# The y^T products of a unit joined to the next unit's first level, a planner that counts changes of product kind, and weight loads that wait on a semaphore

## The chip, the cores and the metric

One core of a Trainium2 chip. The metric is the device time of one launch in microseconds (us); the kernel before has a median of 994.12 us over 3 runs (993.74, 994.12 and 997.86).

## The reference

A recurrent attention over 768 time steps for 4 x 8 heads of width 48, then two feed-forward layers on its 3072 x 384 output, all in float32:

```python
for t in range(S):
    cur = einsum('bhd,bhe->bhde', u[None] * kt, vt)
    y[:, :, t] = einsum('bhd,bhde->bhe', rt, state + cur)
    state = wt[:, :, :, None] * state + einsum('bhd,bhe->bhde', kt, vt)
x = y as (3072, 384)
x = (x @ w_a) * (x @ w_b) @ w_out            # 384 -> 1536 -> 384
h = x @ w_in                                 # 384 -> 2048
out = (max(h, 0) + alpha * min(h, 0)) @ w2_out
```

The weights arrive as 64-bit floats and are made into float32 pairs on the chip.

## The kernel before

**Attention.** The recurrence is cut into 12 units (6 stretches of 128 time steps, two halves of the batch each). In a unit, VectorE builds the products inside blocks of 4, 8 or 16 time steps (`natural`, L577), which go through a small DRAM buffer into the diagonal blocks of a matrix M (`diag`, L642). The blocks beyond the diagonal come level by level: `tree` multiplies decays into the tile Tp on VectorE, and `level` (L682) makes the block products on TensorE into `psl`, which ScalarE copies into M. The first level is h = 4, 8 or 16; from unit 4 on it is 16, with 128 small products, followed by level 32 with 64. Then come `ktrans` (8 transposes into `psk`), `dstate` (64 products into `psd`), the state update, and `yout` (L840): twice 64 products of M and Z into `psx`, the transposed output y^T, one for each half b. ScalarE and VectorE turn each `psx` into the two-part operand X of the first feed-forward layer.

**Feed-forward.** Two units make a block of 512 columns. `mlp1` runs, for each block, 12 steps of nine products into `pa`, nine into `pb` and nine into `acc`, each a 128x128 weight against 512 columns in the reduced float32 format (fp32r). ScalarE copies `pa` out, VectorE multiplies, both split the result. `mlp2` does likewise with the tiles `hp`, `hb` and `acd`. So TensorE does two kinds of product: the attention's small ones in float32, and the feed-forward's large ones in fp32r. In the profile all large ones have line L919.

**Weights.** `load_w` (L412) loads a weight on the Pool queue (`raw`, L432); ScalarE and VectorE make it into `w` (L437 sign, L449 exponent, L443 low part, L452 join, L458 first half, L399 rest). At most 6 loads may be ahead of the making: before a load, GpSimd copies one element of the weight made 6 places earlier into `tick` (L431), and the load stands behind this copy on the Pool queue.

**Order.** Nothing in the code is in its final order. Each piece of work is added to a list with its engine, an estimated duration, a priority, what it reads and writes, and a buffer. `Tasks.run` (L336) simulates the list forwards, takes due times from a backward pass, repeats this 8 times, keeps the order with the earliest simulated end, and issues the pieces in that order; on the chip each engine then works through its own pieces strictly in that order. The accumulators `psk`, `psd`, `psx` and `psl` share a pool of three PSUM banks. Until the first `pa`, idle TensorE time is filled with products of no use (`warm`).

Of the kernel before, what the change touches and what calls it, by code (L numbers as in the profile page):

```python
# [7 lines left out]
F32 = mybir.dt.float32  # L8
# [66 lines left out]
class Tasks:  # L75
# [26 lines left out]
    def add(self, eng, dur, prio, fn, r=(), w=(), alloc=None, nbytes=0, work=0, packet=3072, kind="", late=0.0):  # L102
# [32 lines left out]
            self.late[i] = late  # L135
        return i

    def forward(self, prio):
        import heapq

# [25 lines left out]
        runs = []  # L166
        done = [0.0] * n
        taken = {}

        for i in range(n):  # L170
            if not need[i]:
# [32 lines left out]
        while left:  # L204
            progress = True
            while progress:
                progress = False
                for eng, q in ready.items():
                    if busy.get(eng, 0.0) > now + 1e-9 or not q:
                        continue  # L210
                    q.sort()
                    for k, (p, i) in enumerate(q):
                        if at[i] > now + 1e-9:
                            continue
                        if eng == "PE" and warming() and low(now + t[i][1], self.work.get(i, 0.0)):
                            filler()
                            progress = True
                            break
                        if now < 75.0 and eng in ("ACT", "DVE") and soon(eng, p, t[i][1]):
                            break  # L220
                        al = t[i][5]
                        if al:
                            tag = al[0]
                            if free[tag] <= 0 or tag not in self.ANY and self.pool_seq[tag][nxt[tag]] != i:
                                continue
                            free[tag] -= 1
                            taken.setdefault(tag, []).append(i)
                            nxt[tag] += 1
                        q.pop(k)
                        if eng == "PE":  # L230
                            runs.append((now, now + t[i][1], self.work.get(i, 0.0) / max(t[i][1], 0.01)))
                        start[i] = now
                        order.append(i)
                        if t[i][6]:
                            busy[eng] = now + t[i][1]
                            end = None
                            queues.issue(i, eng, busy[eng], *self.dma[i])
                        else:
                            busy[eng] = end = now + t[i][1]
                        serial += 1  # L240
                        heapq.heappush(ev, (busy[eng], serial, -1))
                        if end is not None:
                            serial += 1
                            heapq.heappush(ev, (end, serial, i))
                        if end is not None:
                            ends[i] = end
                        progress = True
                        break
            if warming() and busy.get("PE", 0.0) <= now + 1e-9:
                filler()  # L250
            landed = queues.next(ev[0][0] if ev else 1e9)
            if landed:
                serial += 1
                heapq.heappush(ev, (landed[0], serial, landed[1]))
                continue
            if not ev:
                raise RuntimeError("stuck")
            now, _, i = heapq.heappop(ev)
            if i >= 0:
                left -= 1  # L260
                done[i] = now
                ends.pop(i, None)
                for h in users.get(i, ()):
                    left_use[h] -= 1
                    if not left_use[h]:
                        free[self.handles[h][0]] += 1
                for s in succ[i]:
                    need[s] -= 1
                    at[s] = max(at[s], now + (
                        self.LAT[t[i][0]] + self.late.get(s, 0.0) if t[s][0] != t[i][0] else self.SAME.get(t[i][0], 0.0)))  # L270
                    if not need[s]:
                        ready.setdefault(t[s][0], []).append((prio[s], s))
                        if at[s] > now:
                            serial += 1
                            heapq.heappush(ev, (at[s], serial, -1))
        return now, start, done, order, taken

    def backward(self, start, done, taken):
# [26 lines left out]
        now, left, serial = 0.0, n, 0  # L305
        wait = []
        while left:
            progress = True
            while progress:
                progress = False  # L310
                for eng, q in ready.items():
                    if busy.get(eng, 0.0) > now + 1e-9 or not q:
                        continue
                    i = heapq.heappop(q)[1]
                    end = now + t[i][1]
                    busy[eng] = end
# [19 lines left out]
    def run(self):  # L336
        t = self.t
        prio = [x[2] for x in t]
        best = None
        for k in range(8):  # L340
            end, start, done, order, taken = self.forward(prio)
            if best is None or end < best[0]:
                best = end, order
            late, span = self.backward(start, done, taken)
            prio = [x + end if i >= self.keep and t[i][2] > -190 else t[i][2] for i, x in enumerate(late)]
            self.__dict__.setdefault("log", []).append((end, span))
        for i in best[1]:
            (t[i][3] if i >= 0 else self.fill[0])()
        return best[0]
# [3 lines left out]
def rwkv_then_moe_kernel(  # L353
# [51 lines left out]
        return n / 1200 + (0.05 if psum else 0.093)  # L405


    W = {}
    prev = []
    WL = int(6)  # L410

    def load_w(key, src, pr, after=()):  # L412
# [12 lines left out]
        def ld():  # L425
            c["raw"] = wp.tile([128, 384, 2], U32, tag="w", name="raw", bufs=NW)
            if gate:
                nc.gpsimd.tensor_copy(tick, first_m[1][96:97, 0, 0, 32:33])
            if behind:

                nc.gpsimd.tensor_copy(tick, W[behind][0:1, 0, 0:1].bitcast(F32))  # L431
            nc.gpsimd.dma_start(out=c["raw"].bitcast(I64).rearrange("p n one -> p (n one)"), in_=src)  # L432

        def sign():

# [19 lines left out]

        def hi():
            W[key] = wp.tile([128, 2, 384], F32R, tag="w", name="w", bufs=NW)
            nc.scalar.copy(W[key][:, 0], c["s"].bitcast(F32))  # L458
# [15 lines left out]
    cur = {}  # L474
    first_m, first_z = {}, {}
    X = {}

    def unit(u, pr):

# [202 lines left out]
        def level(h, bs, p):  # L682
# [27 lines left out]
            def extract(hd):  # L710
# [10 lines left out]
                    else:  # L721
                        nc.scalar.copy(dst, src)  # L722

            add("PE", (1.15 if h == 32 or z == 32 else 1.6 if h == 16 else 1.8) + 0.22 * nf, p, mms, r=nm(f"{T}/r", bs) + nm(f"{T}/k", bs), w=[ps],
                alloc=(pool, ps), work=12 * ms + 512 * nf, late=1.5 if u >= 2 else 0.0)
# [38 lines left out]
        def dstate(p):  # L764
# [21 lines left out]
            add("PE", 1.16 if u > 1 else 2.1, p, run, r=[kn + "/0", kn + "/1", V], w=[f"psd{u}_{i}" for i in range(nd)],  # L786
                alloc=(pool, f"psd{u}_{nd - 1}"), work=672 * nd, late=1.5 if u >= 2 else 0.0)


# [47 lines left out]

                add("ACT", act(384, True), p + 6, begin, r=[f"psd{u}_{cc}"], w=s)

        def yout(b, p):  # L840


            st = {}
# [29 lines left out]
            add("PE", 1.0, p, mms, w=[ps], alloc=(pool, ps), work=2048, late=1.5 if u >= 2 else 0.0,  # L873
                r=[mn(hd, k) for hd in range(2) for k in KM]
                + [zn(cc, hd, k) for cc in range(2) for hd in range(2) for k in "VS"])
            add("ACT", act(384, True), p, hi, r=[ps], w=[f"x{j}/{u}{b}h"], alloc=("x", f"x{j}") if first else None)
            add("DVE", dve(384), p, lo, r=[ps, f"x{j}/{u}{b}h"], w=[f"x{j}/{u}{b}l"])


        if u:  # L880
            loads_v()
        for d in range(C):
            natural(d, pr(-0.1))
        diag(pr(-0.1))
        if not u:
            loads_v()
# [444 lines left out]
```

## Time and profile before

| | before |
|---|---|
| median of 3 runs | 994.12 us |
| profiled execution | 993.15 us |
| its span, first to last instruction | 991.4 us |
| TensorE busy | 978.1 us, 99% of the span |
| VectorE busy | 714.5 us, 72% |
| ScalarE busy | 421.6 us, 43% |
| GpSimd busy | 102.1 us, 10% |
| granted TensorE clock, mean | 0.998 of full speed |

How to read it: PE is TensorE's matmuls, PEld its weight loads (which run beside matmuls), DVE VectorE, ACT ScalarE, POOL GpSimd, SP the engine that only issues DMAs. In a timeline a run of like instructions is one row with its start, the time from its first start to its modelled last end, and its count; since matmuls overlap, the start of the next row is what tells how long a run took.

### The profile page before, as it was taken

The numbers are of one execution on the slowest core, as the hardware profiler recorded it, in microseconds if no ns is written. First come the engines' busy times: TensorE is split into PE (matmuls) and PEld (weight loads), VectorE is DVE, ScalarE is ACT, GpSimd is POOL, SyncE is SP. The second block draws the span as 40 slices with busy tenths as digits, with TensorE's granted clock in tenths as the row PEclk, the third lists the DMA queues.
The fourth block names the chain that finished last, engine by engine and source line by source line (L and its number), as shares of the span: only waits on it lengthen the run. The fifth ranks groups of instructions, "written<-read, shape, count | busy, mean of one in ns | idle before, by whom it ended". The sixth has DMA issues, their size and how long they took to land.

```text
span 991.4 us, 21159 instructions
## 1 busy us (share of the span) xinstructions
PE 978.1 (99%) x8808; PEld 822.5 (83%) x8808; DVE 714.5 (72%) x1215; ACT 421.6 (43%) x919; POOL 102.1 (10%) x173
## 2 busy tenths in 40 slices
PE   7999999999999999999999999999999999999998
PEld 4668788888887887888888888999999999999998
DVE  9989989898988999989726675555454645554543
ACT  0789895535535445362529993111211121211111
POOL 1326421000100000020004321000000000000000
PEclk9999999999999999999999999999999999999999
DMA  7895983314244241443107550020100100000000
GB/s 217 214 249 153 278 182 100 110 39 131 69 113 125 51 134 39 128 124 90 38 27 233 177 160 32 1 64 1 32 33 1 33 32 1 33 1 1 33 1 32
DMA packets 84559, 86.99 MB, mean 88 GB/s; under 512 B 62000, under 2 KB 71344, under 8 KB 83184
## 3 DMA queue, kind: packets, MB, share of 16 engines
q1 hardware_dynamic: 77296, 54.18, 21.1%
q0 software_dynamic: 7168, 31.46, 10.3%
q8 instruction: 69, 1.13, 0.5%
q14 instruction: 26, 0.21, 0.1%
HBM read 73.24 MB, written 11.01 MB: 85 GB/s over the span
## 4 chain that ended last, share of the span: by engine, by line
PE 92%; DVE 2%; ACT 2%; DMA 1%; issue 1%; POOL 0%; SPq 0%; ACTq 0%; POOLq 0%; DVEq 0%
PE acd L919 15%; PE hb L919 15%; PE acc L919 15%; PE pa L919 14%; PE pb L919 14%; PE hp L919 10%; PE psl L704 3%; PE warm L1167 3%; PE psx L857 2%; PE psd L778 1%; DMA raw<-in_wt_dram 1%; PE psk L754 1%; ACT M L722 1%; DVE e L399 1%; DMA idt<-in_ident_dram 0%
## 5 line engine op out<-in xcount | busy, mean ns | idle before, releaser
L919 PE MATMUL acd<-w,g 128*128 128x384 f32 x864 | 192.6, 335 | 0.0
L1101 ACT CAST g<-g 128x512 fp32r<-128x512 f32 x96 | 57.8, 620 | 299.0 <-DVE g L1096 275.3
L919 PE MATMUL acc<-g,w 128*128 128x512 f32 x648 | 174.1, 398 | 0.0
L919 PE MATMUL pa<-x,w 128*128 128x512 f32 x648 | 161.6, 394 | 2.2 <-ACT a L970 2.2
L919 PE MATMUL pb<-x,w 128*128 128x512 f32 x648 | 160.2, 391 | 0.0
L919 PEld LDWEIGHTS acd<-w,g 128*128 128x128 f32 x864 | 154.2, 188 | 1.8
L1092 DVE TENSOR_SCALAR g<-hp,al 128x512 f32<-128x512 f32 x48 | 36.0, 751 | 155.4 <-PE hp L919 155.4
L919 PEld LDWEIGHTS pa<-x,w 128*128 128x128 f32 x648 | 120.9, 188 | 28.9 <-ACT a L970 3.0
L919 PEld LDWEIGHTS pb<-x,w 128*128 128x128 f32 x648 | 120.8, 188 | 25.4 <-DVE a L399 0.2
L919 PEld LDWEIGHTS acc<-g,w 128*128 128x128 f32 x648 | 119.5, 189 | 25.7 <-DVE g L399 0.3
L399 DVE TENSOR_TENSOR Tp<-Tp 112x1024 f32<-112x1024 f32 (+2 forms) x132 | 106.9, 810 | 5.5 <-DMA Tp<-in_rkw_t_dram 4.8
L919 PE MATMUL hb<-x,w 128*128 128x512 f32 x432 | 102.9, 391 | 0.0
L919 PE MATMUL hp<-x,w 128*128 128x512 f32 x432 | 102.0, 389 | 0.0
L919 PEld LDWEIGHTS hp<-x,w 128*128 128x128 f32 x432 | 81.1, 188 | 16.8
L919 PEld LDWEIGHTS hb<-x,w 128*128 128x128 f32 x432 | 80.8, 188 | 16.0
L919 PE MATMUL hb<-w,g 128*128 128x384 f32 x288 | 92.5, 335 | 0.0
L623 DVE TENSOR_REDUCE A<-e 128x16 f32<-128x768 f32 (+15 forms) x148 | 85.9, 580 | 1.0
L981 ACT CAST g<-a 128x512 fp32r<-128x512 f32 x72 | 44.6, 619 | 87.9 <-DVE a L399 78.8
L399 DVE TENSOR_TENSOR g<-g,g 128x512 fp32r<-128x512 f32 x96 | 64.2, 687 | 18.4 <-ACT g L1101 17.6
L399 DVE TENSOR_TENSOR a<-a,pb 128x512 f32<-128x512 f32 x72 | 49.2, 684 | 33.8 <-PE pb L919 33.8
L970 ACT COPY a<-pa 128x512 f32<-128x512 f32 x72 | 41.9, 582 | 62.1 <-PE pa L919 56.9
L399 DVE TENSOR_TENSOR g<-a,g 128x512 fp32r<-128x512 f32 x72 | 49.6, 688 | 14.3 <-ACT g L981 14.1
(83 smaller groups left out, 1099.7 us busy)
## 6 DMA issues: line engine op xcount, KB each, us to landing
raw<-in_wt_dram POOLq DMA_DIRECT2D x68, 384.0 KB, 4.5
Tp<-in_rkw_t_dram SPq DMA_DIRECT2D x33, 448.0 KB, 6.0
N<-in_rkw_n_dram SPq DMA_DIRECT2D x10, 1152.0 KB, 5.3
x2d<-x POOLq DMA_DIRECT2D x36, 128.0 KB, 2.4
x2r<-x2d SPq DMA_DIRECT2D x36, 128.0 KB, 2.3
out_dram<-o SPq DMA_DIRECT2D x24, 192.0 KB, 1.9
V<-in_v_s_dram SPq DMA_DIRECT2D x11, 384.0 KB, 3.5
Z<-in_v_s_dram SPq DMA_DIRECT2D x44, 96.0 KB, 3.2
```

What stands on the lines that cost most here:

```text
L399: nc.vector.tensor_tensor(out=out, in0=a, in1=b, op=op)
L623: nc.vector.tensor_reduce(out=v[:, :, d:d + (n - 1) * (SUB + 1) + 1:SUB + 1], in_=part(st["e"], 0, n), axis=AX.X, op=ALU.add)
L704: nc.tensor.matmul(out=st["ps"][o0:o0 + ms, cc, q, zc * i:zc * i + zc], lhsT=t[b0:b0 + 48, 1, q0 + q, t0:t0 + ms], rhs=r[b0:b0 + 48, q0 + ...
L722: nc.scalar.copy(dst, src)
L754: nc.tensor.transpose(st[g][:, i], cur["T", u][:, 1, 4 * g + i], idt[0:112, 0:112])
L857: nc.tensor.matmul(out=st["ps"][32 * g:32 * g + 32, s // 4, 64 * cc:64 * cc + 64], lhsT=zt(cc, hd)[:, 4 * b + q, c0:c0 + 32], rhs=mt(hd)[: ...
L919: nc.tensor.matmul(out=out, lhsT=lhsT, rhs=rhs, start=start, stop=stop)
L970: nc.scalar.copy(c["a", f], c["pa"])
L981: nc.scalar.copy(c["g", f][:, 0], c["a", f])
L1092: nc.vector.tensor_scalar(out=st["m", f], in0=st["h", f], scalar1=0.0, scalar2=al[:, f:f + 1], op0=ALU.min, op1=ALU.mult)
L1101: nc.scalar.copy(st["g", f][:, 0], st["m", f])
L1167: nc.tensor.matmul(out=warm["ps"][:, 0:512], lhsT=idt, rhs=idt.unsqueeze(1).to_broadcast([128, 4, 128]), start=True, stop=True)
```

## The change

Four things.

1. `yout` no longer adds its products to the list for units 2 to 11; it holds them. For units 2 to 5 and 11, `both_out` adds the two halves as one piece of 128 products. For units 6 to 10 they stay held until the next unit's first `level`, which becomes one piece: 64 + 64 products of y^T, then its own 128. It needs what all three needed, takes three PSUM banks at once, and the copies out of `psx` follow it. In units 7 to 11 the within-block work (`natural`, `diag`, the loads of V and Z) is added after the levels, since it writes M and Z, which the held products still read.
2. The planner counts a change between small and large products as 0.1 us of TensorE, in the forward and the backward pass; durations of small pieces are lowered a little. The sort key of TensorE's ready list gets a term that is 0.0 either way.
3. It takes the best of 24 plans, not 8.
4. A weight load no longer stands behind a copy on GpSimd: the DMA itself depends on the instruction that makes the earlier weight. Its duration in the plan goes from 1.1 to 0.6 us.

```diff
+    def small(self, i):
+        return i in self.work
...
                         else:
                             busy[eng] = end = now + t[i][1]
+                            if eng == "PE" and t[i][1] and self.small(i) != small:
+                                small = not small
+                                busy[eng] = end = end + 0.1
...
-        for k in range(8):
+        for k in range(24):
...
+            ask = nc.gpsimd.dma_start(out=c["raw"].bitcast(I64).rearrange("p n one -> p (n one)"), in_=src)
             if behind:
-
-                nc.gpsimd.tensor_copy(tick, W[behind][0:1, 0, 0:1].bitcast(F32))
-            nc.gpsimd.dma_start(out=c["raw"].bitcast(I64).rearrange("p n one -> p (n one)"), in_=src)
+                dep = mybir.DependencyInfo(mybir.DependencyClass.Sync, mybir.DependencyReason.DATA)
+                tc.add_manual_dep(ask.ins, made[behind].name, dep, reason="weights made")
...
-        add("Pool", 1.1, pr - 40, ld, r=after, w=[raw], alloc=("w", raw), nbytes=128 * 3072)
+        add("Pool", 0.6, pr - 40, ld, r=after, w=[raw], alloc=("w", raw), nbytes=128 * 3072)
...
+            before = held[:]
+            held.clear()
+
+            def run():
+                for x in before:
+                    x[0]()
+                mms()
+
+            for x in before:
+                add("PE", 0.0, p, lambda: None, w=[x[1]], alloc=(x[2], x[1]))
+            add("PE", (1.05 if h == 32 or z == 32 else 1.45 if h == 16 else 1.7) + 0.22 * nf + 0.93 * len(before), p, run,
+                r=nm(f"{T}/r", bs) + nm(f"{T}/k", bs) + [y for x in before for y in x[3]], w=[ps] + [x[1] for x in before],
+                alloc=(pool, ps), work=12 * ms + 512 * nf + 2048 * len(before), late=1.5 if u >= 2 else 0.0)
+            for x in before:
+                x[4]()
...
+            if wait:
+                held.append((mms, ps, pool, reads, leave))
+                return
+            add("PE", 0.92, p, mms, w=[ps], alloc=(pool, ps), work=2048, late=1.5 if u >= 2 else 0.0, r=reads)
+            leave()
...
+        def both_out(p):
+            before = held[:]
+            held.clear()
+            x, y = before
+            add("PE", 0.0, p, lambda: None, w=[x[1]], alloc=(x[2], x[1]))
+            add("PE", 1.85, p, lambda: (x[0](), y[0]()), w=[x[1], y[1]], alloc=(y[2], y[1]), work=4096, late=1.5 if u >= 2 else 0.0, r=x[3])
+            x[4]()
+            y[4]()
...
+        late = bool(held)
+        if not late:
+            natural_way()
         for i, h in enumerate((1, 2, 4, 8, 16, 32)):
...
+        if late:
+            natural_way()
...
-        yout(0, pr(0.8))
-        yout(1, pr(0.85))
-
+        for b in range(2):
+            yout(b, pr(0.8 + 0.05 * b), u >= 2 or 6 <= u < 11)
+
+        if held and not 6 <= u < 11:
+            both_out(pr(0.8))
```

## Rows read from the trace of the kernel before

**Rows 1.** The page, its first part: busy us, share, instructions of each engine.
```profile
PE 978.1 (99%) x8808; PEld 822.5 (83%) x8808; DVE 714.5 (72%) x1215; ACT 421.6 (43%) x919; POOL 102.1 (10%) x173
```

**Rows 2.** Busy time by stretch; last three columns granted clock, DMA share, GB/s.
```profile
113.00:120.30 7.30, 5.24 (x16) 3.87 (x16) 7.18 (x12) 5.76 (x12) 4.18 (x6) 0.77 1.05 368
...
300.00:400.00 100.00, 99.14 (x1287) 80.80 (x1276) 95.06 (x172) 48.69 (x114) 3.21 (x6) 1.00 0.36 94
```

**Rows 3.** Waits of TensorE, whole span: total us, times, longest.
```profile
PE pa L919 <- ACT a L970: 2.2, 1, 2.2
```

**Rows 4.** Timeline of TensorE between unit 5's two y^T runs: start, us, count last.
```profile
247.54 0.96 PE L919 MATMUL acc<-g,w 128*128 128x512 f32 x3
248.44 1.10 PE L857 MATMUL psx<-M,Z 128*32 128x64 f32 x64
```

**Rows 5.** Timeline of TensorE, unit 9's y^T and unit 10's first level.
```profile
424.36 1.99 PE L857 MATMUL psx<-M,Z 128*32 128x64 f32 x128
426.28 0.96 PE L919 MATMUL acc<-g,w 128*128 128x512 f32 x3
427.18 1.22 PE L704 MATMUL psl<-Tp 48*16 48x16 f32 x128
428.32 2.35 PE L919 MATMUL acc<-g,w 128*128 128x512 f32 x9
```

**Rows 6.** Timeline of TensorE, first levels of units 7, 8 and 9.
```profile
299.39 1.32 PE L704 MATMUL psl<-Tp 48*16 48x16 f32 x125
301.08 0.21 PE L704 MATMUL psl<-Tp 48*16 48x16 f32 x3 [0.36 <-issue]
301.22 2.34 PE L919 MATMUL pa<-x,w 128*128 128x512 f32 x9
...
338.74 1.41 PE L704 MATMUL psl<-Tp 48*16 48x16 f32 x128
...
340.08 1.65 PE L919 MATMUL acc<-g,w 128*128 128x512 f32 x6
...
383.80 1.10 PE L857 MATMUL psx<-M,Z 128*32 128x64 f32 x64
384.83 0.57 PE L704 MATMUL psl<-Tp 48*16 48x16 f32 x51
385.90 0.79 PE L704 MATMUL psl<-Tp 48*16 48x16 f32 x77 [0.49 <-issue]
386.62 2.35 PE L919 MATMUL pb<-x,w 128*128 128x512 f32 x9
```

**Rows 7.** DMA queue of instructions (packets, MB, share): whole span, then 383-383.5.
```profile
q8 instruction: 69, 1.13, 0.5%
...
q8 instruction: 1, 0.02, 15.5%
```

**Rows 8.** The chain that ended last, around 100 us: start, us, what.
```profile
99.89 1.44 POOL tick L431
101.33 10.53 DMA raw<-in_wt_dram
```

**Rows 9.** Timelines of ScalarE and TensorE around the wait at 113.
```profile
111.94 0.66 ACT L437 ACTIVATE ws<-raw 128x384 f16<-128x384 f32 x1 [1.40 <-DMA raw<-in_wt_dram]
...
115.06 3.04 PE L919 MATMUL pa<-x,w 128*128 128x512 f32 x9 [2.18 <-ACT a L970]
117.90 2.47 PE L919 MATMUL acc<-g,w 128*128 128x512 f32 x6
120.30 1.99 PE L857 MATMUL psx<-M,Z 128*32 128x64 f32 x128
```

**Rows 10.** Groups by line: GpSimd's copies ahead of loads.
```profile
L431 POOL COPY tick<-w 1x1 f32<-1x1 f32 x62 | 43.9, 707 | 78.8 <-ACT w L458 78.7
```

**Rows 11.** Timeline of TensorE, large products with nothing between them.
```profile
163.27 2.20 PE L919 MATMUL pa<-x,w 128*128 128x512 f32 x9
165.31 2.20 PE L919 MATMUL pb<-x,w 128*128 128x512 f32 x9
```

More of the change, by code (lines that the diff above doesn't have):

```diff
@@ L168, in forward @@
         taken = {}
+        small = True
         for i in range(n):
@@ L210, in forward @@
                         continue
-                    q.sort()
+                    if eng == "PE" and now > 150.0:
+                        q.sort(key=lambda x: (x[0] + (0.0 if self.small(x[1]) != small else 0.0), x[1]))
+                    else:
+                        q.sort()
                     for k, (p, i) in enumerate(q):
@@ L304, in backward @@
                 heapq.heappush(ready.setdefault(t[i][0], []), (key(i), i))
-        now, left, serial = 0.0, n, 0
-        wait = []
+        now, left, small = 0.0, n, False
         while left:
@@ L315, in backward @@
                     end = now + t[i][1]
+                    if eng == "PE" and t[i][1] and self.small(i) != small:
+                        small = not small
+                        end += 0.1
                     busy[eng] = end
@@ L405, in act @@
         return n / 1200 + (0.05 if psum else 0.093)
-    W = {}
+    W, made = {}, {}
     prev = []
@@ L457, in hi @@
             W[key] = wp.tile([128, 2, 384], F32R, tag="w", name="w", bufs=NW)
-            nc.scalar.copy(W[key][:, 0], c["s"].bitcast(F32))
+            made[key] = nc.scalar.copy(W[key][:, 0], c["s"].bitcast(F32)).ins
         def lo():
             tt(W[key][:, 1], c["s"].bitcast(F32), W[key][:, 0].bitcast(F32), ALU.subtract)
-        add("Pool", 1.1, pr - 40, ld, r=after, w=[raw], alloc=("w", raw), nbytes=128 * 3072)
+        add("Pool", 0.6, pr - 40, ld, r=after, w=[raw], alloc=("w", raw), nbytes=128 * 3072)
         yield
@@ L476, in rwkv_then_moe_kernel @@
     X = {}
+    held = []
     def unit(u, pr):
@@ L722, in extract @@
                         nc.scalar.copy(dst, src)
-            add("PE", (1.15 if h == 32 or z == 32 else 1.6 if h == 16 else 1.8) + 0.22 * nf, p, mms, r=nm(f"{T}/r", bs) + nm(f"{T}/k", bs), w=[ps],
-                alloc=(pool, ps), work=12 * ms + 512 * nf, late=1.5 if u >= 2 else 0.0)
+            before = held[:]
[11 more added lines that the diff above has]
+                x[4]()
             for hd in range(2):
@@ L785, in dstate @@
                 add("PE", 0.0, p, lambda: None, w=[f"psd{u}_{i}"], alloc=(pool, f"psd{u}_{i}"))
-            add("PE", 1.16 if u > 1 else 2.1, p, run, r=[kn + "/0", kn + "/1", V], w=[f"psd{u}_{i}" for i in range(nd)],
+            add("PE", 0.98 if u > 1 else 1.9, p, run, r=[kn + "/0", kn + "/1", V], w=[f"psd{u}_{i}" for i in range(nd)],
                 alloc=(pool, f"psd{u}_{nd - 1}"), work=672 * nd, late=1.5 if u >= 2 else 0.0)
@@ L838, in state, with yout @@
                 add("ACT", act(384, True), p + 6, begin, r=[f"psd{u}_{cc}"], w=s)
-        def yout(b, p):
+        def yout(b, p, wait=False):
             st = {}
@@ L872, in yout, with leave, natural_way @@
             first = u == us[0] and b == 0
[L873 to L886, printed above, removed]
+            reads = [mn(hd, k) for hd in range(2) for k in KM] + [zn(cc, hd, k) for cc in range(2) for hd in range(2) for k in "VS"]
+            def leave():
+                add("ACT", act(384, True), p, hi, r=[ps], w=[f"x{j}/{u}{b}h"], alloc=("x", f"x{j}") if first else None)
+                add("DVE", dve(384), p, lo, r=[ps, f"x{j}/{u}{b}h"], w=[f"x{j}/{u}{b}l"])
+            if wait:
[11 more added lines that the diff above has]
+            y[4]()
+        def natural_way():
+            if u:
+                loads_v()
+            for d in range(C):
+                natural(d, pr(-0.1))
+            diag(pr(-0.1))
+            if not u:
+                loads_v()
+        late = bool(held)
+        if not late:
+            natural_way()
         for i, h in enumerate((1, 2, 4, 8, 16, 32)):
```

## The prediction

> **What bounds the kernel.** I read the page's first part, then the stretches, then TensorE's waits, and only then single timelines. TensorE is busy 978.1 of 991.4 us [rows 1], and in a typical attention stretch 99.1 of 100 [rows 2]. So after the start the time is the sum of what TensorE issues, and an edit is worth what it takes from that sum. The waits of TensorE that the profile names in that stage are few: one of 2.2 us on ScalarE's copy of `pa` [rows 3], and 0.36 and 0.49 us in which a level waited for "issue", that is, for nothing the profile shows [rows 6]. Both matter below. VectorE is 95% busy in the same stretch [rows 2], yet TensorE doesn't wait for it there. The sum is made against the profiled run, 993.15 us (span 991.4 and 1.75 around it).
>
> **A change of kind.** Nine large products between large ones take 2.04 us (163.27 to 165.31 [rows 11]), 0.227 each. Three of them between two small runs take 247.54 to 248.44, 0.90 us where 0.68 is due [rows 4]: entering and leaving a small run costs 0.22 us together. Also a run of 64 y^T products takes 1.03 us (383.80 to 384.83 [rows 6]), one of 128 takes 1.92 [rows 5], 0.14 less than two of 64. So one run fewer saves 0.22 + 0.14 = 0.36 us. I use it for y^T joined to a level too, where the trace doesn't show the second part; bounds 0.22 and 0.36.
>
> How many runs go? I walked TensorE's timeline. Units 2, 3, 9 and 10 have their 128 y^T products in one run already (as in [rows 5]); units 4, 5, 6, 7, 8 and 11 have two of 64 (as in [rows 4]), and the second of unit 8 touches unit 9's level [rows 6]. Saved: one each for units 4, 5, 8, 9, 10 and 11, two each for 6 and 7: ten runs, 3.6 us (2.2 at the lower bound). All on the path, since TensorE is the path. The count of changes in the planner adds no order of its own, as its new key term is 0.0 either way; it only alters which of 24 plans looks best. I cost that at nothing, plus or minus 1.5 us (four runs more or fewer by chance).
>
> **The stall that a long run meets.** A first level of 128 products takes 1.14 us when nothing is amiss (427.18 to 428.32 [rows 5]). Unit 7's took 299.39 to 301.22 = 1.83, unit 9's 384.83 to 386.62 = 1.79, unit 8's 338.74 to 340.08 = 1.34 [rows 6]: 0.69, 0.65 and 0.20 too long, 1.5 us together, with TensorE idle for "issue" in the middle of two of them. What for? 69 instruction packets of 1.13 MB [rows 7] carry 8808 matmuls and 8808 weight loads [rows 1]: 255 instructions a packet, some 128 products with their loads. Between the two stalls (301.08 and 385.90 [rows 6]) lie 1019 products by the timeline, eight packets less five products. And one packet is seen just ahead: at 383-383.5 [rows 7], the stalled product following at 385.90, 2.4 to 2.9 us later. So TensorE ran out of instructions: a packet's 128 products last 29 us when they are large, but 1.1 to 1.8 us when they are small, and the next packet takes longer than that.
>
> The joined run is 256 products, two packets' worth, so nearly always a whole packet is used up inside it. Its price comes from the four places where y^T and a level stand closest. Unit 9's level: three large products (0.90 us with the changes) lay in the packet before its stall; without them the stall is 0.65 + 0.90 = 1.5. Unit 7's likewise, 0.69 + 0.90 = 1.6. Unit 8's: nine large products, 0.20 + 2.04 + 0.22 = 2.5, which I cap at 2.0, as the packet's small products also take time. Unit 10's: no stall with three between, so 0 to 0.9, say 0.45. Mean 1.4; five joined runs, 6.9 us. Ends: nothing, and 5 x 2.0 = 10. The 1.5 us of today's stalls is inside these runs and goes: net +5.4.
>
> [...]
>
> **The weight loads.** The copies on GpSimd took 707 ns each, 62 of them [rows 10], and stood in front of the loads. One place in the trace shows what that costs: the chain runs through a copy of 1.44 us at 99.89 and then a load that needed 10.53 us [rows 8], DMA being full (1.05 of 16 engines' time, 368 GB/s [rows 2]). ScalarE waited 1.40 us for it [rows 9]; the copy of `pa` was queued behind on ScalarE, and TensorE idled 2.18 us behind that [rows 9]. Then the clock fell to a mean of 0.77 over the stretch [rows 2]: nine large products took 2.84 us, not 2.04, and six 2.40, not 1.36 plus 0.09 for the change [rows 9, 11], 1.75 us lost. Price of the place: 3.9 us. With the load issued at least 1.44 earlier, ScalarE's 1.40 goes; what is late next is ScalarE's own backlog, 2.18 - 1.40 = 0.78 us of idle, nearer the 0.49 that left the clock alone [rows 6] than 2.18. I take 1.40 + 1.75 = 3.15 us. Ends: 3.9, and none (the plan is new, its order may put another copy late). The wait sits on the DMA instruction now: behind it on the Pool queue stand only further loads and the stores of `x2d`, as before. The later loads feed no wait of TensorE, so there the change is worth nothing.
>
> **Moved work.** y^T of units 6 to 10 waits for the next unit's first level, 3 to 8 us later than now (unit 9: 424.36 to 427.18 [rows 5]). Behind it wait the copies to X, and SP's loads of Z and diagonal blocks. Cover: large products left over from the block before. Where that cover ends, see the third rival.
>
> **Sum.** 993.15 - 3.6 + 5.4 - 3.15 = 991.8. The median of the runs before stands 0.97 above its profiled run, pulled by 997.86; the two others 0.8. I add 0.8: **992.6 us**, within 0.5% of before (half a per cent, about 5 us, is what a measurement can tell here).
>
> **Rivals.** (1) *No stalls in the joined runs*, because packets arrive in time: unit 10's level had none. Then 993.15 - 3.6 - 1.5 - 3.15 + 0.8 = 985.7. For it: 424.36 to 428.32 [rows 5], 256 small products with three large ones between and no loss. Against: [rows 6]. Two or fewer of five stalling comes near it, 988.5. [...] Chance 0.29. (2) *The stall lowers the clock.* A 1.4 us idle lies between 0.49 (clock untouched [rows 6]) and 2.18 (0.77 [rows 2, 9]); if the fall begins below it, four of the five runs cost 1.75 more: 992.6 + 7.0 = 999.6, slower. It decides where a joined run idles over about 1.4 us. Chance 0.08. (3) *X late for the next block.* Blocks 3 and 4 start on y^T of units 7 and 9; the last y^T ended at 426.28, and only three and nine large products and a level stand before the next block. If the level's input comes later than that cover (about 5 us), TensorE idles and the clock falls, 3.9 us a place at the price of 113: 992.6 + 2 x 3.9 = 1000.4. Chance 0.06. (4) *The early wait stays* or comes up elsewhere, all else as forecast: 995.8; chance 0.10, still no change. The forecast itself 0.47.
>
> **Range.** 985.5 (rival 1) to 999 (rival 2 nearly whole); the likeliest case alone 988.5 to 996.5. Faster: rival 1 and a little of the forecast's lower edge, 0.31. Slower: rivals 2 and 3 less those under 5 us, 0.13. Same: 0.56.
>
> **What would show it.** Small runs of 256 in TensorE's timeline with "issue" idles of 1 to 2 us inside, an instruction packet some 2.5 us ahead of each; ten fewer changes of kind; no wait on `a` near 113 and clock 1.00 there; no copies on GpSimd. Wrong if the joined runs take about 3.1 us each (1.92 + 1.14), if the start before the first `pa` at 64 us moves, or if TensorE waits anew on X.

## The result, and where the time went

The changed kernel takes 1004.77 us (median of 6 runs, 1002.1 to 1011.24) against 993.86 us of before (6 runs): ratio 1.0112, 95% interval 1.0086 to 1.0138. It is slower, by 10.9 us, and outside the predicted range. Its profiled execution took 1010.29 us, span 1008.5; it is the second slowest of the six, 5.5 above their median, so the places below add up to more than the median lost.

The page's first part and TensorE's waits (columns as in [rows 1, 3]), of after:

```profile
PE 982.0 (97%) x8810; PEld 825.3 (82%) x8810; DVE 716.7 (71%) x1215; ACT 421.7 (42%) x919; POOL 59.9 (6%) x111
```

```profile
PE psl L717 <- issue: 8.2, 5, 2.2
...
PE psx L883 <- issue: 4.4, 2, 3.0
PE pb L969 <- DVE a L411: 2.1, 3, 1.0
PE pa L969 <- DVE w L411: 0.7, 1, 0.7
PE acc L969 <- ACT g L1031: 0.6, 1, 0.6
```

TensorE's busy time is 3.9 us higher than before [rows 1], though the work is the same but for two products (8810 and 8808): the granted clock fell three times, not once, and each fall cost about 1.7 us (below), which makes 3.4 of it. The wait on ScalarE's `a` [rows 3] is gone, and so are the 62 copies on GpSimd [rows 10]. In their place TensorE waits 12.6 us for "issue", seven times (before 1.4 us, three times), and 2.1 us for VectorE's product `a`.

Three marks divide the two profiled runs. The first `pa` starts at 70.92 us, not 64.07 (+6.9). From there to the first `hp` it is 531.2 us, not 521.6 (+9.5; the stage with the joined runs). From there to the end it is 406.4, not 405.7.

**The joined runs.** TensorE's timeline at three of the five (units 6 to 7, 9 to 10, 10 to 11), with the stalled rows of the two others, which answers to [rows 5, 6]:

```profile
299.62 1.99 PE L883 MATMUL psx<-M,Z 128*32 128x64 f32 x128
301.55 0.38 PE L717 MATMUL psl<-Tp 48*16 48x16 f32 x30
303.14 0.97 PE L717 MATMUL psl<-Tp 48*16 48x16 f32 x98 [1.22 <-issue]
304.04 1.66 PE L969 MATMUL acc<-g,w 128*128 128x512 f32 x6
...
351.00 0.33 PE L717 MATMUL psl<-Tp 48*16 48x16 f32 x24 [1.38 <-issue]
...
397.18 0.78 PE L717 MATMUL psl<-Tp 48*16 48x16 f32 x76 [1.54 <-issue]
...
436.96 1.99 PE L883 MATMUL psx<-M,Z 128*32 128x64 f32 x128
438.89 1.55 PE L717 MATMUL psl<-Tp 48*16 48x16 f32 x128
440.37 2.34 PE L969 MATMUL acc<-g,w 128*128 128x512 f32 x9
...
483.00 1.99 PE L883 MATMUL psx<-M,Z 128*32 128x64 f32 x128
484.93 1.31 PE L717 MATMUL psl<-Tp 48*16 48x16 f32 x122
488.41 0.23 PE L717 MATMUL psl<-Tp 48*16 48x16 f32 x6 [2.17 <-issue]
488.56 0.97 PE L969 MATMUL acc<-g,w 128*128 128x512 f32 x3
489.37 3.81 PE L969 MATMUL pb<-x,w 128*128 128x512 f32 x9
493.02 1.55 PE L969 MATMUL acc<-g,w 128*128 128x512 f32 x6
```

Without a stall a joined run is 1.92 + 1.14 = 3.06 us [rows 5]. These three took 4.42, 3.41 and 5.56; the two others 4.72 (346.54 to 351.26) and 4.77 (393.12 to 397.89). Above 3.06 that is, in order of time, 1.36, 1.66, 1.71, 0.35 and 2.50, mean 1.5. After the longest, nine large products took 3.65 us (489.37 to 493.02) where 2.04 is due. The stretches there (columns as in [rows 2]) say why:

```profile
486.00:488.00 2.00, 0.24 (x28) 0.13 (x15) 1.86 (x5) 0.00 (x0) 0.00 (x0) 1.00 0.54 98
488.00:490.00 2.00, 1.59 (x11) 1.31 (x12) 1.97 (x4) 1.26 (x4) 0.00 (x0) 0.89 0.53 98
490.00:492.00 2.00, 2.00 (x6) 1.58 (x5) 2.00 (x5) 1.69 (x4) 0.00 (x0) 0.50 0.03 8
492.00:494.00 2.00, 2.00 (x8) 1.55 (x8) 1.12 (x4) 0.06 (x1) 0.00 (x0) 0.75 0.00 0
```

Clocks of 0.89, 0.50 (the lowest in this profile) and 0.75 cost (0.11 + 0.50 + 0.25) x 2 = 1.7 us. The profiled run has three such falls, each about 1.7 us: at 66 (0.58 and 0.57 in 66 to 68 and 68 to 70), at 134 (0.65 and 0.50 in 134 to 136 and 136 to 138) and here. Before's has one, at 116 (0.62 and 0.53 in 116 to 118 and 118 to 120, in the stretch of [rows 2]), apart from its last microsecond (0.50).

**The start.** TensorE's timeline ahead of the first `pa`, before, then after:

```profile
45.51 1.20 PE L704 MATMUL psl<-T 48*32 48x32 f32 x64
46.64 0.63 PE L857 MATMUL psx<-m,z 128*32 128x64 f32 x26
47.76 1.79 PE L857 MATMUL psx<-m,z 128*32 128x64 f32 x102 [0.49 <-issue]
...
59.62 2.24 PE L857 MATMUL psx<-M,Z 128*32 128x64 f32 x128
61.79 2.84 PE L1167 MATMUL warm<-idt 128*128 128x512 f32 x6
64.07 2.64 PE L919 MATMUL pa<-x,w 128*128 128x512 f32 x9
```

```profile
44.93 1.63 PE L717 MATMUL psl<-T 48*48 48x32 f32 x64
46.49 1.43 PE L883 MATMUL psx<-m,z 128*32 128x64 f32 x87
50.89 0.77 PE L883 MATMUL psx<-m,z 128*32 128x64 f32 x41 [2.97 <-issue]
...
52.65 1.20 PE L717 MATMUL psl<-T 48*32 48x32 f32 x64
...
64.42 0.27 PE L883 MATMUL psx<-M,Z 128*32 128x64 f32 x2 [1.45 <-issue]
65.10 2.56 PE L883 MATMUL psx<-M,Z 128*32 128x64 f32 x126 [0.40 <-DVE M L733]
67.59 3.89 PE L1217 MATMUL warm<-idt 128*128 128x512 f32 x6
70.92 2.39 PE L969 MATMUL pa<-x,w 128*128 128x512 f32 x8
```

Unit 0's y^T (`psx` from `m`, `z`) now comes ahead of unit 1's last level (`psl` x64 of 48x32, at 45.51 before and at 52.65 after); it waits 2.97 us for instructions. Unit 1's y^T waits again, and the six products of no use behind it run at a mean granted clock of 0.68, before's at 1.00: 3.33 us to the first `pa`, not 2.28.

### The profile page after: what moved, and what is told of

Read it like the earlier page. It is cut to its first block, busy times and chain, and to the rows that moved or that the text cites. A ratio compares the mean times of both kernels' runs of the same rounds, so it can differ in the third digit from the quotient of the medians.

```text
span 1008.5 us, 21028 instructions
## 1 busy us (share of the span) xinstructions
PE 982.0 (97%) x8810; PEld 825.3 (82%) x8810; DVE 716.7 (71%) x1215; ACT 421.7 (42%) x919; POOL 59.9 (6%) x111
## 4 chain that ended last, share of the span: by engine, by line
PE 83%; DVE 8%; DMA 4%; issue 2%; ACT 1%; SPq 0%; DVEq 0%
PE acd L969 15%; PE hb L969 15%; PE pb L969 12%; PE acc L969 11%; PE pa L969 11%; PE hp L969 10%; PE psl L717 4%; PE warm L1217 3%; DVE Tp L411 2%; PE psx L883 2%; DMA Tp<-in_rkw_t_dram 2%; DVE e L411 2%; DVE A L636 1%; DMA N<-in_rkw_n_dram 1%; DVE a L411 1%
```

## The experiments

Each kernel's runs stand against runs of before on the same chip. For the comparison of two kernels I also use each run's mean granted clock c: of a run of T us, (1 - c) x T was lost to the clock, which agrees with the place above (three falls of 1.7 us; 0.005 x 1010 = 5.05). "Rest" is the mean of what is left. Over all 81 runs of before (mean clocks 0.993 to 1.0) the time rises by 1.02 us per 0.001 of clock. The kernels ran on four chips, where the rest of before is 992.2 to 993.0, and a kernel's mean rest is itself uncertain by 0.3 to 1.4; a difference of rests under about 1 us tells nothing.

Four of these kernels, e2_plan, e3_nojoin, e4_both and j_blk, don't compute the reference's result: it is off by a relative 0.16 (e3_nojoin 0.28), and which read or write their order misplaces isn't known. Their times can still show what an order of pieces costs, but a misplaced piece may also have waited too little, so where a conclusion uses one of them, a pair of kernels with the right result is named beside it.

| kernel | runs | median us | ratio, 95% | rest | lost to clock |
|---|---|---|---|---|---|
| before | 81 | 994.35 | | 992.6 | 1.9 |
| after | 6 | 1004.77 | 1.0112, 1.0086 to 1.0138 | 1002.1 | 3.9 |
| e1_sem | 10 | 994.46 | 1.0003, 0.9987 to 1.0019 | 993.0 | 2.0 |
| e2_plan | 4 | 1002.61 | 1.0093, 1.0059 to 1.0127 | 997.5 | 6.3 |
| e3_nojoin | 4 | 1003.93 | 1.0094, 1.0076 to 1.0112 | 999.2 | 4.8 |
| e4_both | 10 | 997.34 | 1.0030, 1.0010 to 1.0050 | 996.1 | 1.0 |
| v_dur | 4 | 1000.43 | 1.0070, 1.0043 to 1.0097 | 998.2 | 2.5 |
| v_c24 | 12 | 992.93 | 0.9988, 0.9974 to 1.0003 | 992.7 | 1.0 |
| b_old | 12 | 993.94 | 1.0006, 0.9989 to 1.0022 | 993.7 | 0.8 |
| j_old | 6 | 1008.11 | 1.0125, 1.0099 to 1.0152 | 1001.7 | 5.9 |
| b_blk | 11 | 992.94 | 0.9980, 0.9968 to 0.9993 | 992.4 | 0.6 |
| j_blk | 4 | 1004.82 | 1.0119, 1.0097 to 1.0140 | 999.6 | 5.8 |
| b_warm | 12 | 993.87 | 0.9991, 0.9978 to 1.0003 | 993.4 | 0.8 |
| b_blkw | 12 | 993.78 | 0.9993, 0.9974 to 1.0012 | 993.1 | 0.8 |

### Is it instructions that a joined run waits for? (e5_shift)

The changed kernel with 40 products of no use ahead of unit 5's first level:

```diff
+                for _ in range(40 if (u, h) == (5, 16) else 0):
+                    nc.tensor.matmul(out=st["ps"][0:16, 0, 0, 0:16], lhsT=t[64:112, 1, 0, 0:16], rhs=r[64:112, 0, 0, 0, 16:32])
```

> The changed kernel with 40 small matmuls more (80 products in the trace's count) at the head of unit 5's first level; they are written over. Everything behind them moves by 80 places against the blocks of 128 products that an instruction packet holds. Theory A (the idle inside a joined run is the wait for the next packet, at the packet's border): the level's products done before the idle, 30, 104, 52 and 122 in the joined runs of units 6, 7, 8 and 10, become 30-80+128 = 78, 24, 100 and 42; with 24 the packet before reaches back into large products, so little or no idle there; unit 9, which had no idle with a border at about 13 of the run, gets one at about product 61 of the level, 1.5 us. Rival E (the level waits for data or for a bank): the idles stay where they were, at 30, 104, 52 and 122. Time within 3 us of the changed kernel's on either.

One run, 1006.23 us. In TensorE's program it is 80 products more (8890 against 8810 in the pages). The second part of each of the five levels in its timeline:

```profile
298.84 0.57 PE L719 MATMUL psl<-Tp 48*16 48x16 f32 x50 [1.68 <-issue]
...
345.30 1.06 PE L719 MATMUL psl<-Tp 48*16 48x16 f32 x104 [1.22 <-issue]
...
392.54 0.37 PE L719 MATMUL psl<-Tp 48*16 48x16 f32 x28 [1.33 <-issue]
...
437.91 0.73 PE L719 MATMUL psl<-Tp 48*16 48x16 f32 x67 [1.78 <-issue]
...
485.21 0.91 PE L719 MATMUL psl<-Tp 48*16 48x16 f32 x86 [1.05 <-issue]
```

With 128 products in a level, the idles come after product 78, 24, 100, 61 and 42. In after they came after 30, 104, 52, none seen, and 122. Each moved by -80 or +48, which is the same thing in steps of 128. What the joined runs read, write and wait for is the same; their place in the instruction stream is not. The fourth run, which was nearly free, got a stall of 1.78. One part of the expectation missed: with the border after product 24 it said little or no idle, and there were 1.22 us. So the stalls are packets of 128 products running out, and which run pays what depends on where the border falls. A packet is seen on the instruction queue 300.5 to 301 us in after, the stalled product following at 303.14, as before [rows 7]. For the run at 436.96, which passed, a packet is seen 435 to 435.5, ahead of the run, and none from 437 to 439. The two rows (packets, MB, share) are

```profile
q8 instruction: 1, 0.02, 12.5%
...
q8 instruction: 1, 0.02, 12.8%
```

That holds in all six profiles of kernels with joined runs (after, after_b, e5_shift, j_old, j_old_b, j_blk). In 22 of their 30 joined runs TensorE idles, and in each of the 22 a packet is first seen inside the run, 2.2 to 2.8 us ahead of the stalled product (in after at 300.7, 348.6, 394.6 and 485.9, 2.3 to 2.6 us ahead). In the eight that pass, a packet is seen 0.3 to 2.6 us ahead of the run. So whether a joined run passes goes with whether its packet was seen before it began.

### Holding and joining (e3_nojoin, e4_both)

e3_nojoin is the changed kernel in which no y^T is held; e4_both holds it, so that both halves are one piece, but never joins it to a level:

```diff
-            yout(b, pr(0.8 + 0.05 * b), u >= 2 or 6 <= u < 11)
+            yout(b, pr(0.8 + 0.05 * b), False)
```

```diff
-        if held and not 6 <= u < 11:
+        if held:
```

> The changed kernel with y^T never held: planner and semaphore stay, each half of y^T is a piece of its own. Its order before the first pa is the changed kernel's. Theory A: first pa near 71; only one place with a y^T run against a level is left, the one of 32 before the first level of unit 3, so about 7 to 9 us of stalls and clock go, and eleven small runs come (60 against 49, 4 us): 999 to 1002 us. Rival C (the joined runs are the whole loss): 992 to 995 us. Rival B: 1000 to 1004.

> The changed kernel with the two halves of y^T always one piece, but never joined to a level. 55 small runs, none of them against another. Theory A: first pa near 71, no idle for instructions inside small runs after it; 996 to 999 us, below the kernel without any holding by 5 runs of 0.36 us and a stall of 2 us at unit 3. Rival C: 990 to 993 us. Rival D (a run of 128 y^T products alone already stalls): as the changed kernel, 1003 to 1006.

e3_nojoin is as slow as after (1003.93, above the 999 to 1002 expected); so the loss isn't the join's alone (v_dur, below, shows that with the right result). In its profile TensorE waits 3.18 us for instructions ahead of 126.02, where unit 2's y^T stands against unit 3's level, and its first `pa` is at 67.53. e4_both is 6.6 us faster than e3_nojoin by the medians; by the means it is 3.1 of the rest and 3.8 of the clock. Joining, e4_both to after, costs 7.4 of the median; by the means 6.0 of the rest and 2.9 of the clock (j_old less b_old, below, is the pair with the right result). This step holds more than the join: where nothing is held from one unit to the next, the within-block work of units 7 to 11 stands ahead of the levels again, as before.

### The planner and the weight loads (e1_sem, e2_plan, v_dur, v_c24)

These take single lines of the change's diff. e1_sem is before with the lines on `ask` and `made` alone, the load's estimate left at 1.1. e2_plan is before with the planner's part alone: the lines on `small`, the estimates, 24 plans; the copies on GpSimd stay. v_c24 is e1_sem with the lines on `small` and 24 plans, v_dur e1_sem with the lowered estimates. The lines of v_dur are

```diff
-            add("PE", (1.15 if h == 32 or z == 32 else 1.6 if h == 16 else 1.8) + 0.22 * nf, p, mms, ...
+            add("PE", (1.05 if h == 32 or z == 32 else 1.45 if h == 16 else 1.7) + 0.22 * nf, p, mms, ...
-            add("PE", 1.16 if u > 1 else 2.1, p, run, ...
+            add("PE", 0.98 if u > 1 else 1.9, p, run, ...
-            add("PE", 1.0, p, mms, w=[ps], ...
+            add("PE", 0.92, p, mms, w=[ps], ...
```

> The kernel before with the weight loads waiting on a semaphore, and nothing else; the estimate of 1.1 us for a load is kept, so that every engine keeps its order. Theory A (the loss of the changed kernel is made of two parts: the new order before the first feed-forward product, and joined runs that run out of instructions; the semaphore is harmless or a gain): the first pa stays near 64 us, the wait of 2.2 us near 113 us is gone or shorter, the time is 990 to 993 us. Rival B (the earlier loads crowd the start and make it late): first pa 3 to 7 us later, time 997 to 1000 us.

> The kernel before with the planner's part alone: changes of kind counted, the lowered durations of small pieces, 24 plans; the y^T pieces as before, the copies on GpSimd as before. Its order of TensorE before the first pa is the changed kernel's but for one fill. Theory A: the first pa near 71 us as in the changed kernel, 7 us late; in three places the plan happens to put a y^T run against a level, two of them long, 1.5 to 2 us each; time 1000 to 1005 us. Rival B (the start is late because of the loads): first pa near 64, time 992 to 997. Rival C (only joined runs cost): the same, 994 to 997.

> The kernel before with loads on a semaphore and the lowered estimates of small pieces; changes of kind not counted, 8 plans, nothing held. By the order printed its start is the changed kernel's. Theory A: first pa at 67 to 71 us, time 997 to 1001 us: the lowered estimates alone cost 4 to 7 us at the start. Rival G (counting and 24 plans, not the estimates, make the planner's loss): 993 to 995 us.

> The kernel before with the semaphore for the weight loads, the count of changes of kind and 24 plans; the lowered estimates of small pieces are left out, and y^T is issued as before. If the planner's cost lies in the lowered estimates (which alone gave 1000.43), this kernel has none of it: TensorE's order up to the first pa is that of before with two fills fewer, first pa at 63 to 66, time 993 to 996. If the count or the choice among 24 plans carries it, 999 to 1003.

The semaphore alone is worth nothing that can be measured (1.0003), and it doesn't make the start late: the first `pa` is at 63.30 us, so rival B is out. TensorE's timeline of e1_sem around the place of [rows 9]:

```profile
113.24 2.35 PE L919 MATMUL pa<-x,w 128*128 128x512 f32 x9 [1.14 <-ACT a L970]
...
121.92 0.75 PE L704 MATMUL psl<-Tp 48*56 48x32 f32 x21 [0.83 <-issue]
122.60 3.66 PE L919 MATMUL pb<-x,w 128*128 128x512 f32 x9
```

The wait went from 2.18 to 1.14 and left the clock alone (1.00 from 113 to 120), as hoped; but 8 us later a stall of 0.83 for instructions inside a level was followed by nine large products in 3.46 us, at granted clocks of 0.82 (122 to 124) and 0.50 (124 to 126). In that profile one stall took the place of another; over ten runs 2.0 us are lost to the clock, as before.

The planner's part alone costs 8.9 us (e2_plan against 993.74 beside it); three long waits for instructions behind the start (1.62, 1.47 and 1.29 us) are part of that. The lowered estimates alone cost 6 (v_dur, rest +5.2 against e1_sem; both with the right result). The count and the 24 plans alone cost nothing (0.9988). It is the lowered estimates that turn TensorE's order round at the start: in v_dur, as in after, unit 0's y^T stands ahead of unit 1's last level. Its timeline there:

```profile
47.48 2.55 PE L857 MATMUL psx<-m,z 128*32 128x64 f32 x87
...
52.54 1.20 PE L704 MATMUL psl<-T 48*32 48x32 f32 x64
...
63.89 0.27 PE L857 MATMUL psx<-M,Z 128*32 128x64 f32 x2 [1.90 <-issue]
...
69.53 2.63 PE L919 MATMUL pa<-x,w 128*128 128x512 f32 x9
```

### The old estimates put back (b_old, j_old, b_blk, j_blk)

Each is the changed kernel: j with the joins, b as e4_both without them; "old" with v_dur's lines reversed throughout (the joined pieces' estimates raised to match), "blk" with the old estimates in units 0 and 1 alone, as here:

```diff
-(1.05 if h == 32 or z == 32 else 1.45 if h == 16 else 1.7)
+((1.15 if h == 32 else 1.6 if h == 16 else 1.8) if u < 2 else 1.05 if h == 32 or z == 32 else 1.45 if h == 16 else 1.7)
```

> The changed kernel with the old estimates of small pieces for units 0 and 1 alone; by the order printed, TensorE's order before the first pa is then that of the kernel before but for one fill, and all joined runs stay. Theory A (the late start comes from the order that the lowered estimates give): first pa at 63 to 65 us, not 68 to 71, and 997 to 1001 us, with the loss that is left in the joined runs and the one y^T run of unit 2 against unit 3's level. Rival C (joined runs are all): as the changed kernel, 1003 to 1006, wherever the first pa is.

> A candidate: the changed kernel with the two halves of y^T as one piece for every unit from 2 on, none joined to a level, and the old estimates of all small pieces; changes of kind counted, 24 plans, loads on a semaphore. 55 small runs, none against another, the old order before the first pa. Theory A: first pa at 63 to 65; four runs fewer (1.4 us), no idle for instructions after the start (1.5 us), the wait at 113 shorter: 989 to 992 us. Rival F (any new plan brings 2 to 5 us of waits on VectorE, as the one with both halves and the lowered estimates had): 993 to 997 us.

> The changed kernel with the old, higher estimates: five runs of y^T joined to a level, and nothing else that b_old (993.94) does not have. If the join costs what its stalls cost, 1.4 to 1.5 us each, the time is 993.94 + 7 = 1001 (999.5 to 1003), with stalls of 1 to 2 us in at least three of the five joined runs. If the join is cheap and the lowered estimates carry the loss, 993 to 996.

> e4_both (997.34) with the old estimates for the first two units alone, so with TensorE's old order up to the first pa. If the 3.4 us between e4_both and b_old come from the start, the time is that of b_old, 993 to 995, and the first pa lies at about 67. If they come from where the later pieces stand, 996 to 998.

Without the joins the loss is gone: 993.94 and 992.94. No gain comes in its place in b_old, for which 989 to 992 had been expected; VectorE is waited for there instead (1.7 us for `a`, 1.2 for `w`, 2.5 for `Tp`). b_blk has the lowest ratio here, 0.2% below before, and differs from e4_both only in the estimates of the first two units: they carry 4.4 us of the median, 3.7 of the rest. With the joins nothing is won back: 1008.11 and 1004.82. For j_blk that refutes theory A, which had 997 to 1001 and a first `pa` at 63 to 65: in its profile the first `pa` is at 69.46, although TensorE's order ahead of it is that of before but for one fill. So with the joins in place the old estimates win 2.5 of the rest in j_blk and 0.4 in j_old, against 3.7 and 5.2 without: the two losses don't add up, and their single sizes depend on what else is in the plan. Three pairs give the price of joining five runs: j_old less b_old is 8.0 of the rest and 5.1 of the clock, j_blk less b_blk 7.2 and 5.2, after less e4_both 6.0 and 2.9; of the first pair both kernels have the right result. I had expected about 1001 of j_old; the clock is what I left out.

### When does a stall lower the clock? (j_old_b, after_b)

The same kernels j_old and after, each profiled once more.

> j_old again, for a profile of a run at a lower mean clock: over its six runs the mean clock went from 0.998 (1003.63, the profiled one) to 0.990 (1012.45), so up to 8 us lie in a clock that falls in some runs and not in others. If it falls behind the stalls of the joined runs, the stretches after them (from about 296, 338, 390, 431 and 480) show large products in two times their 0.227 us each, for 3 to 4 us of every place, and the idle ahead of them is over 1.2 us. If it falls in the start, the stretch before the first pa shows it and those five are at 1.00.

> The changed kernel again, for the same question: which of its stalls lowered the clock in another run. In the first profile (mean clock 0.995) it was the one of 2.17 us ahead of 488.41 and the one of 1.88 at 132.55, and none of those of 1.22, 1.38 and 1.54. If the length of the idle decides, the same two places again; if what TensorE did before it decides or if it is chance, others.

after_b took 1010.84 us at a mean clock of 0.993. j_old_b took 998.59 at 1.0, so it isn't the run at a low mean clock that was wanted; it shows like stalls without a fall. Timelines of after_b (first fence), j_old (third) and j_old_b (fifth) at joined runs, each followed by a stretch there:

```profile
300.76 1.12 PE L717 MATMUL psl<-Tp 48*16 48x16 f32 x98 [1.05 <-issue]
```

```profile
304.00:306.00 2.00, 2.00 (x6) 1.54 (x5) 2.00 (x6) 1.04 (x3) 0.00 (x0) 0.50 0.03 3
```

```profile
484.13 0.22 PE L717 MATMUL psl<-Tp 48*16 48x16 f32 x4 [2.40 <-issue]
```

```profile
484.00:490.00 6.00, 5.87 (x87) 4.76 (x87) 5.61 (x12) 3.72 (x9) 0.00 (x0) 1.00 0.07 13
```

```profile
479.07 0.22 PE L717 MATMUL psl<-Tp 48*16 48x16 f32 x4 [1.86 <-issue]
```

```profile
478.00:484.00 6.00, 4.92 (x50) 3.86 (x51) 5.69 (x12) 3.55 (x8) 0.00 (x0) 1.00 0.25 48
```

In after_b the clock fell behind three of the joined runs' stalls (1.05, 1.80 and 1.35 us); in the first profile of after behind the one of 2.17 alone; in j_old_b behind none, not even 1.86; in j_old's first profile behind 1.75 (ahead of 341.62; 0.73 and 0.50 in 342 to 344 and 344 to 346) but not behind 2.40. The same place with the same kernel goes one way in one run and the other way in the next. So it can fall behind the joined runs, but the length of the idle alone doesn't decide it: of the stalls between 1 and 2.4 us some lowered the clock and some didn't. Over the six profiles with joined runs it fell behind nine of thirty. At 1.7 us each that is 2.6 us a run, near the low end of the 2.9 to 5.2 of the pairs; further falls stand in the start and at unit 3's level (after from 134.59, 0.65 and 0.50 as above; j_blk from 128.42, 0.61 and 0.54 in 128 to 130 and 130 to 132), and that the spread of j_old's runs from 1003.63 to 1012.45 comes from such falls is likely but not shown, as no run of it at a low mean clock was profiled.

### The start's fills (b_warm, b_blkw)

b_old and b_blk have one fill fewer than before ahead of unit 1's y^T, and waited 0.95 and 1.42 us for instructions there. Here it is put back:

```diff
+        warm["n"] = warm.get("n", 0) + 1
+        if warm["n"] == 35:
+            fill()
```

> b_old (993.94) with one fill more ahead of unit 1's y^T, so that TensorE's order up to the first pa is exactly that of before. In b_old's profile TensorE waited 0.95 us for instructions ahead of that run and 0.82 inside it; in before's it waited for nothing there. If the shorter fill makes the wait (the packet is late and the fill covered it), the first of the two goes, up to 0.9 us, and the time is 993 to 994 at most. If the wait comes and goes from run to run with the arrival of packets and loads, nothing changes: two idles of 0.5 to 1 us there again, 993 to 995.5.

> b_blk (992.94, the fastest so far: both halves of y^T as one piece, no joins, old estimates for the first two units) with one fill more ahead of unit 1's y^T, so that the fills up to the first pa are those of before. If that fill covers the wait of 1.42 us for instructions that b_blk showed there, 991.5 to 992.9; if the wait is chance, 992.5 to 994.

Neither median moved by more than it can tell: 993.87 against 993.94, 993.78 against 992.94. The waits were 0.56 us in b_warm's profile, and 0.58 and 0.85 in b_blkw's. An effect of the fill isn't shown. The first `pa` in ten profiles with before's order at the start lies between 63.21 and 69.46, mean 65.6; in seven with the changed order, between 67.53 and 71.84, mean 69.5. Why a y^T there waits 0.5 us in one run and 1.5 in another stays open; the DMA engines are 0.93 busy at 40 to 60 us in before's profile and 0.94 in after's.

## Why the prediction was wrong

Three kernels stand between before and after, one step from each to the next; the rest and the clock of the table add up. The split between the last two steps goes through e4_both; by b_blk and after alone, both with the right result, the two together are +9.7 and +3.2:

| step | rest | clock | predicted |
|---|---|---|---|
| semaphore (before to e1_sem) | +0.4 | +0.1 | -3.15 |
| halves as one piece, count, 24 plans, later estimates (to b_blk) | -0.6 | -1.4 | -3.6 for all ten runs saved |
| estimates of units 0 and 1 (to e4_both) | +3.7 | +0.4 | 0, within 1.5 |
| joining to the level (to after) | +6.0 | +2.9 | +5.4, clock 0 |
| sum | +9.5 | +2.0 | -1.35 |

**The planner.** The step that failed first is "I cost that at nothing, plus or minus 1.5 us". I had looked at the count and the key, which indeed cost nothing (v_c24), and passed over the lowered durations, which I named only as "a little". They changed the order of the first 60 us, where TensorE has idle time to fill and so nothing in a sum of busy time could show it. Without the joins it is 3.7 to 5.2 us of the rest (b_blk to e4_both, e1_sem to v_dur), with them 0.4 to 2.5. The prediction did name the start as what would prove it wrong ("if the start before the first `pa` at 64 us moves"), and gave it no price.

**The stall.** Right in its mechanism, which the shift showed, and near in size: 1.4 us a joined run predicted, 1.5 measured in the profile, and +5.4 net against 6.0, 7.2 and 8.0 in the pairs. The single guesses, 1.6, 2.0, 1.5 and 0.45 for the levels of units 7 to 10, met 1.36, 1.66, 1.71 and 0.35; unit 11's, for which I had only the mean, met 2.50, above the cap of 2.0. That they fell so near is luck in part: the shift moved every one of them. Rival 1, given 0.29, would have had no stall in the joined runs; four of the five stalled in after, and in the six profiles eight of the thirty, as the one at 436.96, passed without an idle.

**The clock.** Rival 2, given 0.08, came true in part: joining lost 2.9 to 5.2 us to the clock in three pairs, where the forecast had none and the rival 7.0. The step that failed is its condition, an idle of "over about 1.4 us": stalls of 1.05 and even 0.83 were followed by a fall, and 1.86 and 2.40 weren't. What decides it stays open; I should have priced it as a share, which was nine of thirty joined runs (four of ten in the two profiles of after). With the same kernel it fell behind three joined runs in after_b (idles of 1.05, 1.80 and 1.35 us) and behind one in after (2.17).

**The weight loads.** The -3.15 didn't come. The wait was cut by 1.04 us in e1_sem, less than ScalarE's 1.40, and the fall of the clock came behind another stall 8 us later. That is rival 4 ("stays or comes up elsewhere"), to which I gave 0.10. The price of a clock fall was right (1.75 predicted, 1.7 measured); that removing one stall removes it was not: in e1_sem's profile a level 8 us later brought the next. In six kernels with the semaphore and no joins (v_c24, b_old, b_blk, b_warm, b_blkw, e4_both) only 0.6 to 1.0 us are lost to the clock, not 1.9, so some of the 1.75 may have come back there; which of their edits did it isn't shown.

**The runs saved.** TensorE's order in after has 49 small runs between the large products, before's 59: ten fewer, as counted. Their 3.6 us can't be read alone. In b_blk, with five of them, the rest is 0.6 below e1_sem, less than 5 x 0.36 = 1.8, but within what start and spread leave open.

**What didn't happen.** Rival 3 (X late for the next block): TensorE waits on no X anywhere in after's table of waits. New are waits on VectorE's `a` (2.1 us), which the prediction hadn't.

In the profiled run, from the first `pa` to the first `hp`, I can place: joined runs +7.6, clock behind one +1.7, a stall of 1.88 with a fall of the clock at 132 to 137 +3.6, new waits +3.4; saved at 113 -3.9, old stalls -1.5, ten runs -3.6. That is +7.3 of 9.5; 2.2 us are not placed.

## What to carry to other kernels

A run of 256 small products was not cheaper here for being long (1.5 us a joined run above 3.06): count instructions per packet (255 here, some 128 products with their loads) and keep enough large products between small runs for the next packet to land (here 2.2 to 2.8 us from its first sight to the product that needed it), or a change of kind saved (0.36 us) is paid four times over. A change in a planner's estimates is a change of the whole order; diff the order it makes, first where engines idle and DMA is busy (here TensorE's first 60 us, DMA 0.93 to 0.94 at 40 to 60), before costing it at nothing. Where a stall may lower the clock by chance, its price is the stall plus a share of 1.7 us (here about a third), and several runs, not one profile, tell the share.

## What the runs showed of the hardware

- A packet of 128 products with their loads is used up by small products in 1.1 to 1.9 us (1.14 a level's, 1.92 those of y^T [rows 5]); in 22 joined runs the stalled product came 2.2 to 2.8 us after a packet was first seen on the queue (in after 300.5 to 301 and 303.14; 485.5 to 486 and 488.41). Joined runs idled 1.05 to 2.40 us for it. In four of the five profiles that have a border near the run's end, that idle was the longest joined one (2.17 after 122 of the level's 128, 2.40 after 124 in j_old); in after_b it was not (1.35).
- The granted clock fell for about 1.7 us worth of work after idles as short as 0.68 us (b_old, ahead of 18.72; from 20.99 on the clock was lower, 0.75, 0.50 and 0.90 in the three stretches of 2 us from 20 to 26) and didn't after one of 2.40 (j_old, ahead of 484.13; 1.00 from 484 to 490); I had taken 0.5 to 2.2 as the bounds of one threshold.
- Three packets of mainly small products in a row (some 350 of the 384 products ahead), with DMA 0.94 busy at 40 to 60, went with a wait for instructions of 2.97 us ahead of 50.89 in after. The longest of all is 3.18 us, ahead of 126.02 in e3_nojoin, where unit 2's y^T products run into a level.
